# A window-attention and GELU block with its gradients on one core: gathers as plain loads, tokens in gather order, transposes moved between DMA and TensorE, and a new order

## The chip, the cores and the metric

One NeuronCore of a Trainium2 chip runs the whole program; the other cores are idle. The metric is the device time of one execution in microseconds (us), as the median of several runs. Beside it stands one execution that the hardware profiler recorded; every duration below comes from that one.

The engines are TensorE (PE, matrix products and transposes, results in PSUM), VectorE (DVE), ScalarE (ACT), GpSimd (POOL) and SyncE (SP, which here only issues DMA transfers). Each engine executes its own instructions strictly in order and waits on semaphores where it needs another's result.

## The reference

The reference computes a transformer block on 2048 tokens of width 512, and its vector-Jacobian product against a given `grad_out`. Everything is bfloat16.

```
ln1 = layernorm(x)                               # no scale, no shift
q, k, v = ln1 @ wqkv                             # 32 heads of 16
logits[s, w] = q[s] . k[s - 2 w] / 4             # w = 0..7: 8 keys, 2 apart, masked below 0
o[s] = sum_w softmax(logits[s])[w] * v[s - 2 w]
h  = x + o @ wo
h2 = h + gelu_tanh(layernorm(h) @ w1 + b1) @ w2 + b2     # F = 1792
return h2, and the gradients of x, wqkv, wo, w1, b1, w2, b2 against grad_out
```

So there is a forward pass (attention, then feed-forward), the backward pass through both, and the weight gradients, which are sums over all 2048 tokens.

## The kernel before, in words

The tokens are cut into four chunks of 512 (c = 0..3). The tensors of a chunk stand in SBUF either token-major (tokens on the 128 partitions) or feature-major (features on the partitions, 512 tokens along the free axis). The program is written as Python functions that record operations (`op`), each with an engine, a planned duration and what it reads and writes. `pl.emit(ORDER, HOMES)` then emits them in the order of a table of numbers, `ORDER`, made offline by a planner from the planned durations and from transfer rates (`DMA_RATE` and the like); `HOMES` is a table of memory addresses. Within an engine the order is therefore fixed, and it is not the order of the code.

- *Forward, attention.* `layernorm` (L315 to L335) normalises a chunk. `p1_proj` (L523) and `p1_v` (L540) project it to q, k and v. `dots` (L400) makes on DVE a product of 128x4096 elements, and TensorE sums it over each head with products of 32 columns (L408). After the softmax, `gather` (L389) fetches for each of 128 partitions 18 neighbouring rows of v, as an indirect DMA on POOL's queue with an index tile `rowi`; partition p then holds a run of tokens with its window. `band` multiplies (L427, DVE, 128x4096 again, `prbo`), sums on TensorE (L436) and writes with ACT (L441, `ost`). The outcome stands in *gather order*: partition p holds tokens 16 apart in groups of four. `unperm` (L451) transposes it on TensorE and puts the tokens back in order while ACT copies it out (L270). `p1_h` (L631, L638) applies `wo` and adds x.
- *Feed-forward.* `p2_h` (L660, L662), the derivative of GELU (`p2_dg`, L683 to L691, mostly DVE), `p2_out` (L706), and `p2_bwd` (L731, L733, L745 and `ln_bwd` L466 to L475). `goT`, the feature-major `grad_out`, and `w1T`, `w2T` come by transposing DMA from DRAM (`xload`, L264).
- *Backward, attention.* `p3_go` transposes the gradient of h on TensorE (L356, `ghT`, out by ACT), multiplies it by the transposed `wo` (L766, `got`) and turns the outcome back to token-major on TensorE (L378), from where it goes to DRAM (`go_d`). `p3_dots` is `dots` again (`prb`), and `p3_bands` runs `gather` and `band` three more times per chunk: `Rq` with `prbq`, `Rv` with `prbv` (which gathers `go_d`), `Rk` with `prbk`. `shift` (L799) copies coefficient rows with four small DMAs each. `p3_gl1` (L844) is the last product before the gradient of x.
- *Weight gradients* (`wg_ffn`, L872): 736 products that TensorE can run whenever their operands are there; the planner puts them between the other work.

Of the kernel before, what the change touches and what calls it, by code (L numbers as in the profile page):

```python
# [10 lines left out]
P = 128  # L11
BF16 = mybir.dt.bfloat16
# [15 lines left out]
DMA_RATE = 345.0  # L28
WIDE_RATE = 380.0
XPOSE_RATE = 215.0  # L30
XPOSE_SB = 170.0
# [27 lines left out]
class Op:  # L59
    __slots__ = ("i", "eng", "us", "lat", "fn", "bufs", "preds", "soft", "dma", "tag", "key", "piece", "stage", "mode", "cls")  # L60


class Plan:
# [21 lines left out]
    def op(self, eng, us, fn, r=(), w=(), dma=None, tag="", soft=(), piece=0.046, mode=0, cls=0, lat=None):  # L85
        o = Op()
        o.i, o.eng, o.us, o.fn, o.dma, o.tag = len(self.ops), eng, us, fn, dma, tag
        o.lat, o.piece, o.stage, o.mode, o.cls = lat, piece, self.stage, mode, cls
# [61 lines left out]
def kernel(  # L150
# [43 lines left out]
    def cst(name, shape, dt=BF16):  # L194
# [8 lines left out]
    mhalf = cst("mhalf", [P, TPC], F32)  # L203
    zrow = cst("zrow", [RPAD, D])
    rowi = cst("rowi", [P, 2], mybir.dt.uint32)
# [7 lines left out]
    ve1, ve2, nm1, nm2, rstd1, rstd2 = (cst(n, [P, NT], F32) for n in ("ve1", "ve2", "nm1", "nm2", "rstd1", "rstd2"))  # L213
    sg_, c0_, sx_ = (cst(n, [P, 2 * NT], F32) for n in ("sg", "c0", "sx"))

    v_t, k_t, q_t, go_t = ([dram.tile([RB, D], BF16, name=f"{n}_d{c}") for c in range(NC)] for n in ("v", "k", "q", "go"))
    ln1_t, o_t = ([dram.tile([CH, D], BF16, name=f"{n}_d{c}") for c in range(NC)] for n in ("ln1", "o"))
    ln2_t = [dram.tile([P, TPC, D], BF16, name=f"ln2_d{c}") for c in range(NC)]
    g_t, gh_t = ([dram.tile([F, CH], BF16, name=f"{n}_d{c}") for c in range(NC)] for n in ("g", "gh"))
    g3_t = [dram.tile([P, max(KEEP, 1), 4, D], BF16, name=f"g{n}_d") for n in "qkv"]  # L220

# [8 lines left out]
    IDENT, PMAT, SUM4, NSUM4, S32B, SMB, IND8, EMAT, MKB, MHALF, ZROW, ROWI = (fx(n, None) for n in (  # L230
        "ident", "pmat", "sum4", "nsum4", "s32", "sm", "ind8", "emat", "mk", "mhalf", "zrow", "rowi"))
    g3_d = [fx(f"g3{i}", t) for i, t in enumerate(g3_t)]
    v_d, k_d, q_d, go_d = ([fx(f"{n}{c}", t) for c, t in enumerate(ts)] for n, ts in (("v", v_t), ("k", k_t), ("q", q_t), ("go", go_t)))
    ln1_d, ln2_d, o_d = ([fx(n, t) for t in ts] for n, ts in (("ln1", ln1_t), ("ln2", ln2_t), ("o", o_t)))
    g_d, gh_d = ([fx(n, t) for t in ts] for n, ts in (("g", g_t), ("gh", gh_t)))
# [5 lines left out]
    GATHER = 7.0  # L241
# [12 lines left out]
    def load(dst, ap, src_ap, kb, r=(), key=None, tag="load", soft=(), row=1, q="SP"):  # L254
        return op(q, 0.5, lambda: (SY if q == "SP" else A).dma_start(out=ap(), in_=src_ap()), r=r, w=[(dst, key)],
                  dma=kb / (DMA_RATE if row == 1 else WIDE_RATE), tag=tag, soft=soft, piece=0.006 + 0.0385 * row, mode=4)

    def store(dst, ap, src, src_ap, kb, key=None, skey=None, q="SP", tag="store", row=1):
        e, us = (SY, 0.45) if q == "SP" else (G, 0.6)
        return op(q, us, lambda: e.dma_start(out=ap(), in_=src_ap()), r=[(src, skey)], w=[(dst, key)] if dst is not None else (),  # L260
                  dma=kb / (DMA_RATE if row == 1 else WIDE_RATE), tag=tag, piece=0.006 + 0.0385 * row, mode=5)

    def xload(dst, ap, src_ap, kb, r=(), key=None, tag="xload", soft=(), sb_src=False):
        return op("SP", 0.4, lambda: SY.dma_start_transpose(out=ap(), in_=src_ap()), r=r, w=[(dst, key)],  # L264
                  dma=kb / (XPOSE_SB if sb_src else XPOSE_RATE), tag=tag, soft=soft, piece=0.02, mode=3)

# [8 lines left out]

    def consts():
# [4 lines left out]
        op("DVE", 0.1, lambda: V.memset(mhalf[:], -0.5), w=[MHALF], tag="k")  # L281
        op("DVE", 0.27, lambda: V.memset(zrow[:], 0.0), w=[ZROW], tag="k")
        op("ACT", 0.25, lambda: A.copy(out=_sub(Pmat[:], [[1, 8], [8, DH]]), in_=_sub(ident[:], [[DH, 8], [1, DH]])), r=[IDENT], w=[PMAT], tag="k")
        for j in range(4):
            op("ACT", 0.2, lambda j=j: A.copy(out=S32[32 * j:32 * j + 32, :], in_=ident[32 * j:32 * j + 32, 32 * j:32 * j + 32]),
               r=[IDENT], w=[(S32B, j)], tag="k")
# [10 lines left out]
        for g in range(4):  # L297
            op("ACT", 0.2, lambda g=g: A.copy(out=Emat[:, g, 8 * g:8 * g + 8], in_=ind8[:]), r=[IND8], w=[EMAT], tag="k")
        op("POOL", 0.3, lambda: G.memset(mk[:], 0.0), w=[MKB], tag="k")
        for hf in range(2):  # L300
            op("POOL", 0.3, lambda hf=hf: G.affine_select(out=mk[:, hf], in_=mk[:, hf], compare_op=ALU.is_ge, fill=NEG, base=-2 * hf,
                                                          pattern=[[-4, 4], [0, 32]], channel_multiplier=1), w=[(MKB, hf)], tag="k")
        for w4 in range(4):
            for b_, o in ((0, 4 * w4), (1, 4 * (3 - w4))):
                op("POOL", 0.12, lambda w4=w4, b_=b_, o=o: G.iota(rowi[32 * w4:32 * w4 + 32, b_:b_ + 1], pattern=[[0, 1]], base=o * D,
                                                                 channel_multiplier=16 * D), w=[(ROWI, (w4, b_))], tag="k")

    def layernorm(c, src, MV, ST, VE, NM, R, mv, st, ve, nm, rs, dst, eng, tag, per=TPC):
        for g0 in range(0, TPC, per):
            js = range(g0, g0 + per)  # L310
            for j in js:
# [9 lines left out]
            op("DVE", 0.08, lambda s=s: V.tensor_scalar(out=ve[:, s], in0=mv[:, s, 1], scalar1=EPS, scalar2=None, op0=ALU.add),  # L321
               r=[(MV, t) for t in ts], w=[(VE, k)], tag="ve" + tag)
            op("POOL", 1.1, lambda s=s: G.tensor_tensor(out=rs[:, s], in0=ve[:, s], in1=mhalf[:, 0:per], op=ALU.pow), r=[(VE, k), MHALF],
               w=[(R, t) for t in ts], tag="pow" + tag)
# [3 lines left out]
            for j in js:  # L328
# [5 lines left out]
                else:  # L334
                    op("DVE", 0.31, lambda t=t, j=j: V.tensor_scalar(out=dst()[:, j, :], in0=src()[:, j, :], scalar1=mv[:, t, 0:1],  # L335
                                                                    scalar2=rs[:, t:t + 1], op0=ALU.subtract, op1=ALU.mult),
                       r=[(src, j), (R, t), (MV, t)], w=[(dst, j)], tag="norm" + tag)
# [5 lines left out]
    def to_fm_dma(src, dst, tag):  # L343
        xload(dst, lambda: _sub(dst()[:, 0, 0:1], [[P, 16], [1, P]]), lambda: src().rearrange("p j d -> p (j d)"), 512, r=[src], tag="fm" + tag,
              sb_src=True)
# [833 lines left out]
```

## Time and profile before

| what | number |
|---|---|
| median of three runs | 582.69 us (581.72 to 582.99) |
| the profiled execution, its own time | 582.41 us |
| its span, first to last instruction | 580.6 us |
| mean granted TensorE clock | 0.994 |
| TensorE busy | 554.3 us, 95% of the span |
| VectorE busy | 495.6 us, 85% |
| ScalarE busy | 340.9 us, 59% |
| GpSimd busy | 57.1 us, 10% |
| data moved by DMA | 133.31 MB |

The span leaves 1.8 us of the profiled execution's time outside it. "Busy" of TensorE contains modelled ends, so a busy TensorE may still have lost cycles; the distance from the start of one run of like instructions to the start of the next tells what one of them costs when nothing disturbs it. Rows of windows give for a stretch of time the busy time of each engine, the number of instructions in brackets, and the clock granted to TensorE (PEclk, 1.00 is full speed).

### The profile page before, as it was taken

To read this page: it belongs to the slowest core of one execution; us is meant where nothing else is said; L and a number is where in the kernel's file an instruction comes from. 1 tells how busy PE (TensorE), PEld (TensorE's weight loads), DVE (VectorE), ACT (ScalarE), POOL (GpSimd) and SP (SyncE) were. 2 spreads that over 40 slices of the span, in tenths; PEclk is the share of its full clock that TensorE was granted. 3 is DMA by queue.
4 is the path that set the end of the run, shared out by engine and by line. 5 is a ranking of instruction groups with operands and counts; after the bars stand their busy time and mean duration, and the time that the engine had idled before them with its cause. 6 is when DMAs were issued, how large, how long until landed. Compare 5 with 4: busy or idle time off the path is not lost.

```text
span 580.6 us, 9061 instructions
## 1 busy us (share of the span) xinstructions
PE 554.3 (95%) x3516; PEld 258.6 (45%) x3516; DVE 495.6 (85%) x649; ACT 340.9 (59%) x508; POOL 57.1 (10%) x67
## 2 busy tenths in 40 slices
PE   4989999799999998999999999999999999999997
PEld 1444444244444443444445445443444445544443
DVE  7789997889999999989997889899788996936824
ACT  5889699689975697669414455121552453542452
POOL 3010125030020113000001000010101001010000
PEclk9999999799999999999999999999999999999999
DMA  9787779688768936877977997869989896997653
GB/s 263 174 278 227 255 225 333 184 135 187 192 231 223 254 115 163 265 154 243 255 244 155 263 202 183 281 217 238 370 170 364 280 263 206 306 333 262 209 182 99
DMA packets 173467, 133.31 MB, mean 230 GB/s; under 512 B 116529, under 2 KB 167793, under 8 KB 171377
## 3 DMA queue, kind: packets, MB, share of 16 engines
q1 hardware_dynamic: 169488, 89.75, 60.0%
q0 software_dynamic: 3936, 42.99, 20.5%
q8 instruction: 27, 0.44, 0.3%
q14 instruction: 16, 0.12, 0.1%
HBM read 59.38 MB, written 42.93 MB: 176 GB/s over the span
## 4 chain that ended last, share of the span: by engine, by line
PE 50%; DVE 5%; DMA 3%; issue 1%; ACT 1%; SPq 1%; ACTq 0%; DVEq 0%
PE ps L872 22%; PE ps L844 7%; PE ps L745 4%; PE ps L731 3%; PE ps L436 3%; PE ps L766 2%; PE ps L706 2%; DMA Rk<-q_d,rowi 2%; DVE prbk L427 2%; PE ps L451 2%; PE ps L408 1%; PE ps L660 1%; DMA gw1in<-gh_d 1%; PE ps L378 1%; PE ps L356 1%
## 5 line engine op out<-in xcount | busy, mean ns | idle before, releaser
L660 PE MATMUL ps<-ln2T,w 128*128 128x512 bf16 x224 | 53.1, 379 | 0.5 <-DVE xb L733 0.2
L706 PE MATMUL ps<-w,gl 128*128 128x512 bf16 x224 | 52.5, 380 | 1.0 <-DVE h2s L708 0.7
L731 PE MATMUL ps<-goT,w2T 128*128 128x512 bf16 x224 | 52.8, 379 | 0.0
L872 PE MATMUL ps<-gw1in,ln2b 128*128 128x512 bf16 (+1 forms) x256 | 51.4, 353 | 0.9 <-DMA gw1in<-gh_d 0.9
L745 PE MATMUL ps<-w1T,xb 128*128 128x512 bf16 x224 | 50.6, 379 | 1.4 <-ACT gyr L466 1.4
L872 PE MATMUL ps<-gor,gw2in 128*128 128x512 bf16 x224 | 51.8, 379 | 0.0
L427 DVE TENSOR_TENSOR prbv<-Rv,cfv 128x4096 bf16<-128x4096 bf16 x16 | 35.9, 2284 | 17.6 <-DMA Rv<-go_d,rowi 13.9
L844 PE MATMUL ps<-wqkvT,gqkvT 128*128 128x512 bf16 x192 | 45.6, 379 | 0.3 <-ACT gqkvT L270 0.3
L662 ACT ACTIVATE xb<-ps,b1c 128x512 bf16<-128x512 f32 x56 | 35.6, 692 | 16.9 <-PE ps L660 15.2
L270 ACT CAST wgs<-ps 128x512 bf16<-128x512 f32 (+1 forms) x30 | 16.4, 566 | 49.5 <-PE ps L872 49.5
L427 DVE TENSOR_TENSOR prbq<-Rq,cfq 128x4096 bf16<-128x4096 bf16 x16 | 36.1, 2283 | 8.5 <-DMA Rq<-k_d,rowi 4.0
L427 DVE TENSOR_TENSOR prbk<-Rk,cfk 128x4096 bf16<-128x4096 bf16 x16 | 36.0, 2284 | 6.7 <-DMA Rk<-q_d,rowi 3.7
L427 DVE TENSOR_TENSOR prbo<-Ro,cfo 128x4096 bf16<-128x4096 bf16 x16 | 36.2, 2276 | 5.6 <-issue 4.9
L466 ACT ACTIVATE gyr<-ps,rstd 128x512 bf16<-128x512 f32 x32 | 21.8, 681 | 28.9 <-PE ps L844 15.7
L400 DVE TENSOR_TENSOR prf<-qt,kt 128x4096 bf16<-128x4096 bf16 x16 | 35.8, 2276 | 3.2 <-ACT qt L270 2.9
L733 DVE SCALAR_TENSOR_TENSOR xb<-xb,ps 128x512 bf16<-128x512 bf16 x56 | 36.8, 679 | 0.7 <-issue 0.2
L270 ACT COPY gqkvT<-ps 128x1024 bf16<-128x1024 bf16 x24 | 24.0, 1019 | 22.6 <-PE ps L451 9.2
L400 DVE TENSOR_TENSOR prb<-got,vw 128x4096 bf16<-128x4096 bf16 x16 | 36.0, 2284 | 0.7 <-PE ps L408 0.6
L872 PEld LDWEIGHTS <-ln2b 128*128 128x128 bf16 x256 | 24.2, 98 | 25.7 <-issue 3.0
L745 PEld LDWEIGHTS <-xb 128*128 128x128 bf16 x224 | 21.9, 98 | 27.7 <-issue 1.7
L706 PEld LDWEIGHTS <-gl 128*128 128x128 bf16 x224 | 21.5, 98 | 28.2 <-issue 3.0
L523 PE MATMUL ps<-ln1T,wqk 128*128 128x512 bf16 x128 | 32.8, 406 | 1.3 <-DMA wqk<-in_A_wqkv_dram 1.1
(170 smaller groups left out, 1009.1 us busy)
## 6 DMA issues: line engine op xcount, KB each, us to landing
g_d<-gl SPq DMA_DIRECT2D x12, 512.0 KB
gh_d<-xb SPq DMA_DIRECT2D x12, 512.0 KB
ln_d<-ln SPq DMA_DIRECT2D x8, 512.0 KB
w<-in_B_w_dram SPq DMA_DIRECT2D x2, 1792.0 KB
out_dram<-wgs SPq DMA_DIRECT2D x13, 256.0 KB
v_d<-tmv SPq DMA_DIRECT2D x8, 256.0 KB
k_d<-tmk SPq DMA_DIRECT2D x8, 256.0 KB
q_d<-tmq SPq DMA_DIRECT2D x8, 256.0 KB
```

The costliest lines, as they stand in the source:

```text
L270: fn = lambda: A.copy(out=ap(), in_=pap())
L400: op("DVE", tt_us(4096), lambda g=g, pr=pr: V.tensor_tensor(out=pr(), in0=ql()[:, g, :].unsqueeze(1).to_broadcast([P, W, 512]), in1=_sub(k ...
L427: V.tensor_tensor(out=pr().rearrange("p a j (d h) -> p a j d h", h=H), in0=_sub(R()[:, o0, 0:1], [[st, 2], [512, 4], [32, DH], [1, H]]), i ...
L523: T.matmul(ps()[:, gg * 512:(gg + 1) * 512], lhsT=wqk()[:, dc, sel * D + g * P:sel * D + (g + 1) * P], rhs=cols(st_[c]["ln1T"], dc, c in F ...
L660: T.matmul(ps(), lhsT=w1()[:, dc, f * P:(f + 1) * P], rhs=cols(ln2T[c], dc, c in FM2), start=(dc == 0), stop=(dc == DC - 1))
L662: op("ACT", act_us(512, 1), lambda f=f, ps=ps, xb=xb, f0=f0: A.activation(out=xb()[:, f - f0, :], in_=ps(), func=ACT.Identity, bias=b1c[:, ...
L706: T.matmul(ps(), lhsT=d["g"][f // 4]()[:, f % 4, j * P:(j + 1) * P], rhs=w2()[:, f, :], start=(f == 0), stop=(f == FT - 1))
L731: T.matmul(ps(), lhsT=w2T()[:, dc, f * P:(f + 1) * P], rhs=goT()[:, dc, :], start=(dc == 0), stop=(dc == DC - 1))
L733: op("DVE", 0.61, lambda f=f, ps=ps, z=z, f0=f0: V.scalar_tensor_tensor(out=z()[:, f - f0, :], in0=z()[:, f - f0, :], scalar=1.0, in1=ps() ...
L745: T.matmul(ps(), lhsT=d["d"][f // 4]()[:, f % 4, j * P:(j + 1) * P], rhs=w1T()[:, f, :], start=(f == 0), stop=(f == FT - 1))
L844: T.matmul(ps(), lhsT=d["gqkv"]()[:, b, j * P:(j + 1) * P], rhs=wqkvT()[:, b, :], start=(i == 0 and b == ks[0]), stop=(i == 2 and b == ks[ ...
L872: T.matmul(ps()[:, 0:N], lhsT=l, rhs=r, start=(n == 0), stop=(n == k - 1))
```

## The change

Line numbers in this section, where they differ, are those of the changed kernel.

- `gather` (L424) is a plain DMA on POOL's queue, whose source pattern names the 128 overlapping runs of 18 rows; the index tile and its eight `iota` are gone. The order of the partitions is mirrored in `dots` and `shift`.
- Tokens stay in gather order after the attention. `turn` (L484) does the same eight transposes as `unperm`, and ACT's copy behind them is contiguous. x is loaded a second time, in gather order (16 loads of 128 KB); `grad_out`, `ln1` and the stores of the outputs are cut in four pieces per chunk in that order; the reciprocal deviations of `ln1` are rearranged through DRAM (one store, four loads, four small DVE copies).
- `ghT`, the token-major gradient of the attention's output (`tmgod`) and `goT` are made by transposing DMA from SBUF to SBUF. 64 + 64 transposes on TensorE and 16 ACT copies of 1024 elements go.
- `w1T` and `w2T` are made by TensorE (`wturn`, L1057): 112 transposes and 14 ACT copies of 1024 elements; eight transposing loads go.
- `shift` is 32 ACT copies of 32 x 1024 elements in place of 32 DMAs.
- For the last chunk, g and the gradient of the hidden layer are transposed from SBUF to SBUF and do not pass through DRAM; the second copies of `ln1` and `ln2` are not stored and reloaded, and `KEEP` (chunks of attention gradients parked in DRAM) is 1 in place of 2.
- The first chunk's layernorm uses ACT's square root and a DVE reciprocal in place of POOL's power; half of its transposes are copied out by DVE.
- `warm` (L290) multiplies zeros 16 times, 128x512.
- The planner's rates are others, and `ORDER` and `HOMES` are new.

The first place is TensorE's queue near the start. Before: `wqk` and `wv` are the projections' weights, `Pmat` turns q to token-major.

```order
L523 LDWEIGHTS wqk_9_187
L523 MATMUL ps<-ln1T_69_10_196,wqk_9_187 128x512
...
L378 LDWEIGHTS qt_94_14_248
L378 MATMUL ps<-Pmat,qt_94_14_248 128x16x8
...
L540 LDWEIGHTS ln1T_69_10_196
L540 MATMUL ps<-wv_16_276,ln1T_69_10_196 128x512
```

After, the same place (`wz` is the tile of zeros; the last pair sums the first DVE product):

```order
L580 LDWEIGHTS ln1T_52_8_172
L580 MATMUL ps<-wv_9_179,ln1T_52_8_172 128x512
...
L397 LDWEIGHTS qt_88_14_234
L397 MATMUL ps<-Pmat,qt_88_14_234 128x16x8
L290 LDWEIGHTS wz_2_116
L290 MATMUL ps<-wz_2_116 128x512
...
L580 LDWEIGHTS ln1T_52_8_172
L580 MATMUL ps<-wv_9_179,ln1T_52_8_172 128x512
...
L440 LDWEIGHTS Emat
L440 MATMUL ps<-prf_16_318,Emat 32x512
```

The 16 products of zeros stand behind the 16 transposes of the first layernorm, 44 projection products and 8 transposes of q; four more products and the first sums follow.

The second place is POOL's queue in the forward attention. Before (`o_d` is the attention's output in DRAM):

```order
L389 DMA Ro_29_573<-v_d_57,rowi 128x9216
L260 DMA o_d_77<-ost_30_668 128x1x512
L389 DMA Ro_26_845<-v_d_58,rowi 128x9216
L323 TENSOR_TENSOR rstd<-ve,mhalf 128x4
L260 DMA o_d_77<-ost_30_668 128x1x512 x3
L389 DMA Ro_31_1108<-v_d_59,rowi 128x9216
L323 TENSOR_TENSOR rstd<-ve,mhalf 128x4
L260 DMA o_d_78<-ost_30_985 128x1x512 x2
```

After:

```order
L424 DMA Ro_14_368<-v_d_57 128x1x9216
L343 TENSOR_TENSOR rstd<-ve,mhalf 128x4
L266 DMA o_d_81<-ost_29_615 128x2048
L424 DMA Ro_27_859<-v_d_59 128x1x9216
L343 TENSOR_TENSOR rstd<-ve,mhalf 128x4
L424 DMA Ro_22_1060<-v_d_58 128x1x9216
L266 DMA o_d_83<-ost_25_1093 128x2048
```

The gathers stay on POOL's queue; chunk 2 is fetched ahead of chunk 1, and a chunk's output leaves in one store.

The third place is TensorE where the backward attention begins. Before (`prb` is the first backward product of DVE; `gw2in` feeds a weight gradient):

```order
L872 LDWEIGHTS gw2in_45_2668
L872 MATMUL ps<-gor_37_2874,gw2in_45_2668 128x512
L356 LDWEIGHTS ghr_1179_39_2944
L356 MATMUL ps<-ident,ghr_1179_39_2944 128x128
...
L872 LDWEIGHTS gw2in_45_2668
L872 MATMUL ps<-gor_44_2432,gw2in_45_2668 128x512
...
L408 LDWEIGHTS S
L408 MATMUL ps<-prb_36_3035,S 32x512
```

After:

```order
L957 LDWEIGHTS xw2in_41_2917
L957 MATMUL ps<-gor_42_2510,xw2in_41_2917 128x512
L841 LDWEIGHTS woT_46_2994
L841 MATMUL ps<-ghT_42_3278,woT_46_2994 128x512
...
L841 MATMUL ps<-ghT_45_3286,woT_46_2994 128x512
L440 LDWEIGHTS S
L440 MATMUL ps<-prb_45_3314,S 32x512
```

Ahead of the first sum of `prb` stood 28 products of weight gradients and 16 of `ghT` with `woT`; now 128 and 32 stand there. The number of TensorE products in the program is 3516 in both.

The core of the diff:

```diff
-DMA_RATE = 345.0
-WIDE_RATE = 380.0
-XPOSE_RATE = 215.0
-XPOSE_SB = 170.0
+DMA_RATE = 325.0
+WIDE_RATE = 337.0
+XPOSE_RATE = 180.0
...
+    def warm(n):
+
+        z = sb("wz", [P, 512])
+        pz = ps_("pwz")
+        op("DVE", 0.2, lambda: V.memset(z(), 0.0), w=[z], tag="wz")
+
+        def mm():
+            for _ in range(n):
+                T.matmul(pz(), lhsT=z()[:, 0:P], rhs=z(), start=True, stop=True)
+        op("PE", 0.2157 * n, mm, r=[z], w=[pz], tag="warm")
...
+            if per == 1:
+                op("ACT", 0.25, lambda s=s: A.activation(out=ve[:, s], in_=mv[:, s, 1], func=ACT.Sqrt, bias=epsc[:]), r=[(MV, t) for t in ts] + [EPSC],
+                   w=[(VE, k)], tag="sd" + tag, mode=7)
+                op("DVE", 0.08, lambda s=s: V.reciprocal(out=rs[:, s], in_=ve[:, s]), r=[(VE, k)], w=[(R, t) for t in ts], tag="rc" + tag)
...
+    def tm_dma(fm, off, dst, c, back, tag, pm):
+
+        st = sb("tm" + tag + "d", [P, 4, 512])
...
+            xload(st, lambda: _sub(st()[:, 0, 0:1], [[P, 16], [1, P]]), lambda: fm().rearrange("p g t -> p (g t)"), 512, r=[(fm, 0), (fm, 1)], tag="tmx" + tag)
+            store(dst[c], lambda: dst[c]()[r:r + CH, :].rearrange("(a p) (g d) -> p g a d", p=P, g=4), st,
+                  lambda: st().rearrange("p g (a d) -> p g a d", d=P), 720, key=0, tag="tmst" + tag, row=0.25)
...
-            G.indirect_dma_start(out=R().rearrange("p a d -> p (a d)"), out_offset=None,
-                                 in_=_ap(t[0:1, :], [[RW * D, RB // RW], [1, RW * D]]),
-                                 in_offset=bass.IndirectOffsetOnAxis(ap=rowi[:, int(back):int(back) + 1], axis=1),
-                                 element_offset=(RPAD - 14 if back else 0) * D)
...
+        op("POOL", 0.58, lambda: G.dma_start(out=R().rearrange("p a d -> p (a d)"), in_=_ap(d_b()[r0:r0 + 1, :], [[4 * D, 4], [16 * D, 32], [1, RW * D]])),
...
-        evict(dst, lambda: _sub(dst()[:, k0, 0:1], [[CH, 4], [16, 32], [1, 8]], 8 * mp), pt,
-              lambda: _sub(pt.bf(), [[256, 4], [1, 32], [32, 8]]), 1024, key=dkey, tag="un" + tag)
+        evict(dst, lambda: dst()[:, 2 * mp:2 * mp + 2, :], pt, lambda: pt.bf().rearrange("p (a n) -> p a n", a=2), 1024, key=mp, tag="un" + tag)
...
-        xload(goT, lambda: goT(), lambda: gof[c * CH:(c + 1) * CH, :], 512, tag="goT", soft=[(d["g"][1], None)])
...
+            load(gor, lambda j=j: gor()[32 * j:32 * j + 32], lambda ap=ap: ap, 128, key=j, tag="gor", soft=[(d["g"][1], None)])
+        to_fm_dma(gor, goT, "go")
...
+        if c in FMG:
+            to_fm_dma(gh_[c], ghT, "gh", soft=[(st_[NC - 1]["d"][2], None)])
...
+        if SHA:
+            for w4 in range(4):
+                op("ACT", act_us(1024), lambda w4=w4: A.copy(out=sh()[32 * w4:32 * w4 + 32],
...
+    def wturn(dst, dap, src, sap, kb, key, tag):
+
+        pt = ps_("ptw" + tag)
+
+        def tr():
+            for k in range(8):
+                T.transpose(pt.bf()[:, k * P:(k + 1) * P], sap(k), ident[:])
+        op("PE", 8 * XP, tr, r=[src, IDENT], w=[pt], tag="xp" + tag)
+        evict(dst, dap, pt, lambda: pt.bf().rearrange("p (a n) -> p a n", a=kb), 1024, key=key, tag="ev" + tag)
...
-KEEP = 2
+KEEP = 1
...
+WARM = 16
+FMG = (0, 1, 2, 3)
...
+SBX = ((0, 3), (1, 3))
+SHA = True
+W2PE = True
+W1PE = True
 ORDER = (
-    29, 25, 26, 4, 8, 11, 13, 12, 1, 9, 2, 6, 30, 32, 7, 79, 0, 20, 21, 22, 23, 5, 27, 56,
...
```

More of the change, by code (lines that the diff above doesn't have):

```diff
@@ L556, in p1_qkv @@
         p1_v(c)
-        to_tm_store(kt, PAD, k_d, c, True, "k", True)
-        to_tm_store(qt, 0, q_d, c, False, "q", True)
+        for fm, o, dd, back, n in ((kt, PAD, k_d, True, "k"), (qt, 0, q_d, False, "q")):
+            (tm_dma if (n, c) in TMD else to_tm_store)(fm, o, dd, c, back, n, c not in QKP)
     def p1_attn(c):
@@ L930 @@
     N2 = [["ACT"] * 4] * 4
+    warm(WARM)
     p1_load(0)
```

350 lines of the change are left out of this document (214 added, 136 removed), and 248 rows, old and new, of tables (HOMES, ORDER).

## The prediction, made before the changed kernel was run

> **What bounds the kernel now.** I read first the page's busy times, then the windows of a whole stage each, then the timeline of the one window that stood out, then the waits of the tiles that arrive by gather. The windows (start and end, length, then each engine's busy time; the last columns are the granted clock, the DMA share and GB/s):
>
> ```profile
> PE 554.3 (95%) x3516; PEld 258.6 (45%) x3516; DVE 495.6 (85%) x649; ACT 340.9 (59%) x508; POOL 57.1 (10%) x67
> ```
>
> ```profile
> 0.00:20.00 20.00, 11.31 (x45) 4.91 (x46) 13.77 (x45) 10.88 (x24) 6.78 (x22) 1.00 0.94 242
> 20.00:100.00 80.00, 75.84 (x598) 36.09 (x596) 76.45 (x72) 70.91 (x95) 15.54 (x10) 1.00 0.79 249
> 100.00:120.00 20.00, 16.04 (x109) 6.31 (x108) 15.76 (x18) 15.10 (x16) 1.74 (x1) 0.83 0.75 185
> 102.00:112.00 10.00, 6.04 (x53) 2.14 (x50) 8.06 (x6) 5.61 (x6) 0.00 (x0) 0.69 0.43 144
> 112.00:225.00 113.00, 112.76 (x595) 50.96 (x592) 108.99 (x186) 92.11 (x112) 16.97 (x17) 1.00 0.78 198
> 180.00:315.00 135.00, 132.43 (x658) 60.60 (x651) 125.12 (x239) 85.33 (x127) 9.74 (x10) 1.00 0.78 205
> 315.00:549.00 234.00, 231.35 (x1645) 110.79 (x1644) 194.01 (x149) 94.94 (x166) 17.45 (x18) 1.00 0.88 260
> 549.00:581.00 32.00, 27.58 (x163) 12.68 (x161) 12.75 (x30) 12.41 (x27) 0.00 (x0) 0.99 0.38 128
> ```
>
> TensorE is the bound over the whole (554.3 of 580.6 us), but not alone. From 20 to 315 us DVE is about as full (76.45 of 80, 108.99 of 113, 125.12 of 135), so there TensorE follows DVE and a delay of either moves the end. From 315 to 549 DVE has 40 us to spare (234 less 194.01), and only TensorE's work counts. The idle time of TensorE is 26.3 us: 8.69 at the start, 4.16 from 20 to 100, 3.96 from 100 to 120, some 5 in the middle, 4.42 at the end.
>
> One window is bad, 100 to 120. Its rows, POOL, DVE and TensorE (start, duration, line; in brackets the idle time before and what ended it):
>
> ```profile
> 60.18 1.14 POOL L389 DMA_INDIRECT Ro<-v_d,rowi  x1 [0.33 <-issue]
> 86.03 8.69 POOL L389 DMA_INDIRECT Ro<-v_d,rowi  x1 [8.64 <-PE ps L436]
> ```
>
> ```profile
> 96.73 2.28 DVE L400 TENSOR_TENSOR prf<-qt,kt 128x4096 bf16<-128x4096 bf16 x1
> 103.94 2.29 DVE L427 TENSOR_TENSOR prbo<-Ro,cfo 128x4096 bf16<-128x4096 bf16 x1 [4.93 <-issue]
> ```
>
> ```profile
> 106.88 1.21 PE L408 MATMUL ps<-prf,Emat 128*32 128x512 bf16 x8 [3.96 <-DVE h L638]
> ```
>
> The gather of chunk 2 takes 8.69 us on POOL where the one before took 1.14. So its rows land late, DVE stands 4.93 us, TensorE 3.96, and for ten microseconds its clock is granted at 0.69. DVE ran its 128x4096 products while POOL was held.
>
> What one instruction costs comes from starts in the tail, where TensorE runs undisturbed:
>
> ```profile
> 557.84 0.61 PE L451 MATMUL ps<-ident,gks 128*128 128x128 bf16 x8
> 558.28 1.03 PE L844 MATMUL ps<-wqkvT,gqkvT 128*128 128x512 bf16 x4
> ...
> 566.92 3.62 PE L872 MATMUL ps<-gq3in,rl 128*128 128x512 bf16 x16
> 570.37 1.89 PE L872 MATMUL ps<-gks,rl 128*128 128x512 bf16 x8
> ```
>
> Eight transposes take 0.44 us, 0.055 each; sixteen products of 128x512 take 3.45 us, 0.216 each.
>
> **The change part by part.** The sum is made against the profiled execution's 582.41 us; the median of the runs is 0.28 above it.
>
> *Gathers.* POOL's own rows:
>
> ```profile
> L389 POOL DMA_INDIRECT Ro<-v_d,rowi x4 | 12.0, 3006 | 46.6 <-PE ps L731 36.9 <-PE ps L436 8.6 <-POOL rowi L305 0.7
> L260 POOL DMA_DIRECT2D o_d<-ost x16 | 10.5, 669 | 49.2 <-ACT ost L441 49.2
> ```
>
> A plain DMA on POOL takes 0.67 us in the mean here, beside the same DVE products, and none of the sixteen is shown long. I take it that the plain gather does the same. Then chunk 2's rows are there in time, and the window from 100 to 120 loses what its neighbours lose. It loses 3.96 us idle and, at 0.69 clock over 6.04 us of work, about 1.9 more; the neighbour from 20 to 100 idles 4.16 in 80, so 1.05 in 20. Gain: 3.96 + 1.9 - 1.05 = 4.8. Bounds: 0, if the plain load is held likewise, and 5.9. The queue's order matters less: the twelve later gathers took about 1 us on POOL, off the path.
>
> [...]
>
> *Start.* Here is what the first projection waited for:
>
> ```profile
> 6.48 0.40 PE L356 MATMUL ps<-ident,ln 128*128 128x128 bf16 x2 [6.48 <-DVE ln L335]
> ...
> 11.17 9.93 PE L523 MATMUL ps<-ln1T,wqk 128*128 128x512 bf16 x32 [1.08 <-DMA wqk<-in_A_wqkv_dram]
> ```
>
> The layernorm loses four POOL powers and one of two ACT copies goes to DVE, but the last release was the weights' load, which the new order puts ahead of the later chunks' x. Gain 0.5, between -0.5 (the square root needs its table first) and 1.5.
>
> *Zeros.* The first 32 products took 9.93 us instead of 32 x 0.216 + 0.16 = 7.1: 2.9 are lost to a slow first stretch. The zeros stand behind these products, so they can't shorten it. They cost 16 x 0.216 = 3.45 us of TensorE. Cover would be DVE: it is nearly full from 20 us on, and TensorE idles 4.16 us up to 100. Loss: 1.0, bounds 0 and 3.45; if they delay the first sums and DVE's product buffers fill, it is the upper one. [...]
>
> *Transposes.* TensorE loses 128 and gains 112 of 0.055: 0.9 gained. ACT loses 16 copies of 1024 elements and gains 14, and 32 for `shift`:
>
> ```profile
> L270 ACT COPY gqkvT<-ps 128x1024 bf16<-128x1024 bf16 x24 | 24.0, 1019 | 22.6 <-PE ps L451 9.2
> ```
>
> 30 x 1.02 = 30.6 us; ACT goes from 340.9 to about 371 of 580, and most of it falls behind 315 us, where ACT works 94.94 of 234. Costed at 0. The eight DMA transposes for `ghT` and `tmgod` occupy SP for 1.9 us each:
>
> ```profile
> L264 SPq DMA_TRANSPOSE ln1T<-ln x3: 1938/1941/1957, 16.1 to 47.5; - x3
> ```
>
> Their cover is 100 products of weight gradients now placed ahead. The bytes fall: 7.3 MB for the last chunk's g and its gradient, 4 for `ln2`, 2 for `ln1`, 3 for one `KEEP`, less 2 for the second x, so some 14 of 133 MB. No term; it shortens landings if anything.
>
> *New order, first part (20 to 315 us).* Ahead of the first sum of `prb` stand 128 weight-gradient products and not 28, and 16 more products of `ghT`: 116 x 0.216 = 25 us of work that needs nothing of DVE, in the stretch where TensorE followed DVE. TensorE's idle time there, without the bad window, is about 4.16 + 0.24 + 2.57 = 7.0, and these fill it in part: I take 4.5. Bounds 0 and 7.0.
>
> *New order, second part (315 to 549).* The same 25 us, and the 72 transposes (4.0 us) that stood behind that point before, are missing there: the stretch shrinks from 234 to 205 us if TensorE sets it, beside DVE's 194. The slack of DVE falls from 40 to about 11 us. What it was spent on:
>
> ```profile
> L427 DVE TENSOR_TENSOR prbv<-Rv,cfv 128x4096 bf16<-128x4096 bf16 x16 | 35.9, 2284 | 17.6 <-DMA Rv<-go_d,rowi 13.9 <-ACT gyr L466 2.8 <-PE ps L436 0.9
> L427 DVE TENSOR_TENSOR prbq<-Rq,cfq 128x4096 bf16<-128x4096 bf16 x16 | 36.1, 2283 | 8.5 <-DMA Rq<-k_d,rowi 4.0 <-PE ps L436 3.8 <-PE ps L766 0.5
> L427 DVE TENSOR_TENSOR prbk<-Rk,cfk 128x4096 bf16<-128x4096 bf16 x16 | 36.0, 2284 | 6.7 <-DMA Rk<-q_d,rowi 3.7 <-issue 3.0
> ```
>
> DVE waited 21.6 us for gathers (13.9 + 4.0 + 3.7). Much of that was DVE running ahead, which it can't now. I take a loss of 2; bounds 0 and 15 (21.6 - 11, and some 4 for late transposes).
>
> Sum: 582.41 - 4.8 - 0.5 + 1.0 - 0.9 - 4.5 + 2.0 = 574.7, and 0.3 for the median: **575**.
>
> **The rivals.**
>
> *DVE binds the second part.* If all 21.6 us of waits stay and only 11 are free, 10.6 are lost in place of 2, and each late `ghT` or `go_d` adds: before, TensorE could turn these itself in 0.44 us per eight, now a transfer stands between two products, four times. With 15 lost: 588; with 20, 593. It turns the verdict from about 10 us of loss on, that is when DVE's waits behind 315 us pass some 20 us. For it speaks that waits of 21.6 were there with more slack; against it that fewer bytes move and that the last waits of TensorE in that stretch were only 2.65 us.
>
> *The plain load is held too.* The 4.8 fall away: 580, still faster. For it: the 8.69 us stood on POOL's queue, where the gathers remain. Against: the plain stores above.
>
> *All of it fits.* TensorE's idle time in the middle goes (7.0), the second part loses nothing, the zeros are covered: 582.7 - 5.9 - 1.0 - 0.9 - 7.0 = 568, or 564 with a better start and tail.
>
> *The change nets nothing.* Zeros fully paid (3.45), no gain from the order, 2 lost behind: 582.7 - 4.8 - 0.5 - 0.9 + 3.45 + 2 = 582, no change.
>
> **How the numbers follow.** Forecast (570 to 579) 0.46; the plain load held (579 to 581.5) 0.10; all fits (562 to 570) 0.07; nothing 0.05; DVE binds the second part (584 to 595) 0.32. 0.2%, 1.2 us, is about what a measurement of this kernel can tell from no change. Faster 0.46 + 0.10 + 0.07 = 0.63, same 0.05, slower 0.32. The range 563 to 592 leaves out a few per cent at the lower end and the worst third of the slower case; the forecast's own range is 570 to 579.
>
> **What would show it.** Right: no POOL row of a gather above 2 us; no window of 20 us with a clock under 0.95 between 20 and 560; TensorE's idle time from 20 to 315 under 4 us without the bad window; the zeros' 3.45 us with DVE not waiting behind them for `prf`; DVE's idle time behind 315 us near 11 and TensorE's there under 5. Wrong: TensorE waiting for `prb`, `prbq`, `prbv` or `prbk` by more than 5 us together, or for `ghT`; a gather of 8 us again; TensorE idle ahead of the zeros.

## The result, and the profile after

The changed kernel takes 977.03 us (974.38 to 984.64, four runs) where the kernel before took 582.21 us beside it: a ratio of 1.680, 95% interval 1.671 to 1.690. The prediction said 575, faster, with a range that ended at 592. It missed by 402 us, in sign and in size. In this section and the next, ratios and intervals leave out executions that ran at a lower clock than the others of the same kernel, while the times beside them are medians of all.

The page of the profiled execution (span 972.6 us) shows first that the engines' work hardly changed:

```profile
PE 585.1 (60%) x3516; PEld 264.4 (27%) x3516; DVE 498.7 (51%) x656; ACT 371.8 (38%) x541; POOL 29.8 (3%) x40
```

DVE is busy 498.7 us, as before (495.6); ACT 371.8, where 371 was forecast; TensorE 585.1 where it was 554.3, at a mean granted clock of 0.805 and not 0.994. So the 392 us by which the span grew are waiting. What DVE waited for (total, times, longest):

```profile
DVE prbv L459 <- DMA Rv<-go_d: 123.0, 4, 34.9
DVE prbq L459 <- DMA Rq<-k_d: 110.1, 4, 39.8
DVE prbo L459 <- DMA Ro<-v_d: 67.4, 2, 33.8
DVE prbk L459 <- issue: 40.9, 2, 36.0
```

It waited 300 us for three of the four kinds of gather alone, some 30 us at a time and up to 39.8. The page's list of DMA issues tells why (the last column is the median time from issue to landing):

```profile
Ro<-v_d POOLq DMA_DIRECT2D x4, 2304.0 KB, 43.5
Rq<-k_d POOLq DMA_DIRECT2D x4, 2304.0 KB, 47.9
Rv<-go_d POOLq DMA_DIRECT2D x4, 2304.0 KB, 42.9
Rk<-q_d POOLq DMA_DIRECT2D x4, 2304.0 KB, 45.1
```

A gather of 2304 KB lands in 43 to 48 us. In the kernel before it landed in about 10; here are the least, the median and the most of its `Ro` gathers:

```profile
DMA to landing us min/median/max: 10.2/10.3/17.8
```

The 17.8 is the gather that POOL held for 8.69 us. In the changed kernel the issue on POOL is as short as forecast (0.67 us each for the later ones); the transfer behind it is four times as long. While the first gather is in flight there is a stretch in which no compute engine of the core works at all. The windows of that stretch and of the two stages around it:

```profile
20.00:100.00 80.00, 45.94 (x370) 22.52 (x368) 40.24 (x40) 40.85 (x52) 3.22 (x4) 0.81 0.59 154
60.00:75.00 15.00, 0.00 (x0) 0.00 (x0) 0.00 (x0) 0.00 (x0) 0.00 (x0) 0.50 0.20 56
315.00:420.00 105.00, 104.80 (x486) 47.21 (x485) 94.19 (x177) 77.10 (x103) 2.36 (x1) 1.00 0.67 158
560.00:760.00 200.00, 73.24 (x427) 30.14 (x425) 57.28 (x37) 39.56 (x61) 3.85 (x6) 0.67 0.88 104
```

From 60 to 75 us every compute engine is at 0.00, and the 16 DMA engines are busy for a share of 0.20, moving 56 GB/s. A fifth of sixteen engines is the work of about three; the view is a mean and does not say which engines they are. Where no gather is needed, 315 to 420 us, TensorE is full (104.80 of 105). The backward attention, 560 to 760, has it busy 73 of 200 us.

The gather also holds transfers that have nothing to do with it. SP's queue and ACT at the first and the second gather:

```profile
35.27 40.22 SPq L261 DMA_DIRECT2D wo<-in_A_wo_dram  x1
```

```profile
138.25 1.01 ACT L276 CAST tmv<-ps 128x1024 bf16<-128x1024 f32 x1 [31.36 <-DMA q_d<-tmq]
```

SP stands 40.22 us on one issue, until the gather has landed, and with it everything behind it in SP's order. The length follows the gather: the same issue stands 28.03 us in k8, 10.85 in k128 and 9.54 in f_indirect, three of the kernels below. ACT waits 31.36 us until an unrelated store has left its tile. The rows show both delays; what makes these transfers wait for the gather they do not show.

One part did better than forecast. TensorE and DVE at the start:

```profile
9.28 5.81 PE L562 MATMUL ps<-ln1T,wqk 128*128 128x512 bf16 x16 [0.25 <-ACT ln1T L276]
```

```profile
16.88 2.26 DVE L432 TENSOR_TENSOR prf<-qt,kt 128x4096 bf16<-128x4096 bf16 x1
```

The first projection begins at 9.28 us (11.17 before) and DVE's first product at 16.88 (20.45 before).

### The profile page after: what moved, and what is told of

Same layout as the page of the kernel before. It is cut to its first block, busy times and chain, and to the rows that moved or that the text cites. A ratio compares the mean times of both kernels' runs of the same rounds, so it can differ in the third digit from the quotient of the medians.

```text
span 972.6 us, 9021 instructions
## 1 busy us (share of the span) xinstructions
PE 585.1 (60%) x3516; PEld 264.4 (27%) x3516; DVE 498.7 (51%) x656; ACT 371.8 (38%) x541; POOL 29.8 (3%) x40
## 4 chain that ended last, share of the span: by engine, by line
DMA 28%; PE 17%; SPq 7%; DVE 2%; issue 2%; ACT 0%; another core or an unknown queue 0%; DVEq 0%; POOLq 0%
DMA Rq<-k_d 10%; DMA Rv<-go_d 9%; PE ps L957 9%; SPq L270 6%; DMA ro<-o_d 5%; DMA Rk<-q_d 4%; PE ps L931 2%; DVE prbq L459 2%; PE ps L841 1%; PE ps L817 1%; PE ps L468 1%; PE ps L803 1%; PE ps L484 1%; SPq L266 1%; PE ps L440 0%
## 5 line engine op out<-in xcount | busy, mean ns | idle before, releaser
L957 PE MATMUL ps<-gw1in,ln 128*128 128x512 bf16 (+1 forms) x192 | 44.9, 383 | 63.7 <-DMA gw1in<-gh_d 63.7
L468 PEld LDWEIGHTS <-S 128*32 128x32 bf16 x512 | 12.0, 104 | 250.0 <-DVE prbo L459 66.9
L721 PE MATMUL ps<-ln2T,w 128*128 128x512 bf16 x224 | 56.8, 399 | 29.1 <-DMA ln2T<-ln 28.9
L468 PE MATMUL ps<-prbv,S 128*32 128x512 bf16 x128 | 12.2, 506 | 82.2 <-DVE prbv L459 82.2
L473 ACT ACTIVATE gvs<-ps 128x512 bf16<-128x512 f32 x16 | 9.4, 605 | 128.3 <-PE ps L468 128.3
L957 PEld LDWEIGHTS <-ln 128*128 128x128 bf16 x256 | 26.1, 105 | 92.4 <-issue 71.5
L468 PE MATMUL ps<-prbo,S 128*32 128x512 bf16 x128 | 11.1, 459 | 65.9 <-DVE prbo L459 65.9
L931 PE MATMUL ps<-wqkvT,gqkvT 128*128 128x512 bf16 x192 | 49.4, 399 | 0.0
L957 PE MATMUL ps<-gor,gw2in 128*128 128x512 bf16 x168 | 39.9, 379 | 1.9 <-DVE xb L805 1.9
L721 PEld LDWEIGHTS <-w 128*128 128x128 bf16 x224 | 21.9, 102 | 58.8 <-issue 37.4
## 6 DMA issues: line engine op xcount, KB each, us to landing
Ro<-v_d POOLq DMA_DIRECT2D x4, 2304.0 KB, 43.5
```

Of the source, the lines that this page charges most:

```text
L468: T.matmul(ps()[32 * j:32 * j + 32, :], lhsT=S32[:], rhs=pr()[:, hf, j, :], start=(hf == 0), stop=(hf == 1), skip_group_check=True)
L721: T.matmul(ps(), lhsT=w1()[:, dc, f * P:(f + 1) * P], rhs=cols(ln2T[c], dc, c in FM2), start=(dc == 0), stop=(dc == DC - 1))
L931: T.matmul(ps(), lhsT=gT()[:, j, b * P:(b + 1) * P], rhs=wqkvT()[:, k0 + b, :], start=(i == 0 and b == 0), stop=(i == 2 and b == 3))
L957: T.matmul(ps()[:, 0:N], lhsT=l, rhs=r, start=(n == 0), stop=(n == k - 1))
```

## The experiments

The question splits in two: what makes a gather four times slower, and what the rest of the change is worth without that. The edits below are to the changed kernel, to *f_indirect* (the changed kernel with the old gather) or to the kernel before, as each says. Ratios are to the kernel before, run on the same chip.

### What slows the gather

The suspect was the shape of the source pattern, `[[4*D, 4], [16*D, 32], [1, RW*D]]`: its outermost dimension counts 4. The rivals were the overlap of the runs in a plain load, and the new transposing DMAs.

*f_four*: the same load in four pieces, each with 32 outermost.

```diff
-G.dma_start(out=R(), in_=_ap(d_b()[r0:...], [[4*D, 4], [16*D, 32], [1, RW*D]]))
+for a in range(4):
+    G.dma_start(out=R()[32*a:32*a+32], in_=_ap(d_b()[r0+4*a:...], [[16*D, 32], [1, RW*D]]))
```

> The changed kernel with each gather cut into four plain loads of 32 partitions, whose outermost source dimension is 32 and not 4; everything else stays. Theory A (a load is spread over no more DMA engines than its outermost dimension counts, so 4 of 16 here): the last of the four lands within 10 to 13 us, DVE's waits for gathers fall from 303 us to under 30, and the time is 565 to 585 us. Theory B (plain loads whose runs overlap are slow however they are written): landing stays above 35 us, time above 900. Theory C (the new transposing DMAs starve the gathers): landing above 30 us, time above 850.

*f_indirect*: the old way of fetching, in the new order of partitions.

```diff
-G.dma_start(out=R(), in_=_ap(d_b()[r0:...], [[4*D, 4], [16*D, 32], [1, RW*D]]))
+G.indirect_dma_start(out=R(), in_=_ap(d_b(), [[RW*D, RB//RW], [1, RW*D]]),
+                     in_offset=IndirectOffsetOnAxis(ap=rowi[:, 0:1], axis=1), element_offset=r0*D)
```

> The changed kernel with the indirect gather put back in the new partition order; everything else stays. A and B: landing near 10 us, time 565 to 585 us, and POOL may again be held for 8 us once or twice. C: landing stays above 30 us, time above 850.

*k8* and *k128*: the changed kernel, where only the counts of the pattern differ.

```diff
-[[4 * D, 4], [16 * D, 32], [1, RW * D]]
+[[4 * D, 8], [32 * D, 16], [1, RW * D]]     # k8
+[[4 * D, 128], [1, RW * D]]                 # k128
```

> The plain load of the changed kernel with 8 as its outermost source dimension and 16 behind it: the same bytes from the same 540 rows, but the tokens reach other partitions, so the attention's outputs are others. A: landing near 21.5 us, half of 43, and a time of 640 to 760 us. B and C: landing stays at 40 to 48 us, time 950 to 1000.

> The plain load of the changed kernel with 128 as its outermost source dimension, neighbouring partitions 4 rows apart: the same bytes from the same rows, other tokens on the partitions, so the attention's outputs are others. Theory A (as many engines as the outermost dimension allows, 16 at most): landing 10 to 13 us and a time of 585 to 597 us, like the indirect gather. Theory B (plain loads of overlapping runs are slow): landing above 20 us, time above 650.

*b_plain4*: the kernel before, with nothing of the change but this load.

```diff
-G.indirect_dma_start(out=R(), ..., in_offset=IndirectOffsetOnAxis(ap=rowi[:, int(back):int(back)+1], axis=1), ...)
+G.dma_start(out=R(), in_=_ap(t[r0:r0+1, :], [[4*D, 4], [16*D, 32], [1, RW*D]]))
```

> The kernel before with the changed kernel's plain load and nothing else of the change; the partitions of the gathers of v and k come in mirrored order, so the outputs are others. A and B: landing near 43 us and a time of 850 to 1050 us. C: landing near 10 us, time 575 to 590.

What was measured. The landing of the `Ro` gathers (least, median, most), in order for the changed kernel, b_plain4, k8, k128 and f_indirect:

```profile
DMA to landing us min/median/max: 42.8/43.5/46.5
```

```profile
DMA to landing us min/median/max: 42.1/44.7/47.2
```

```profile
DMA to landing us min/median/max: 24.4/27.3/30.2
```

```profile
DMA to landing us min/median/max: 8.9/9.7/11.6
```

```profile
DMA to landing us min/median/max: 9.7/10.0/16.9
```

| kernel | outermost count | landing of `Ro`, median us | time, us |
|---|---|---|---|
| changed | 4 | 43.5 | 977.03 |
| b_plain4 | 4 | 44.7 | 940.36 (one run) |
| k8 | 8 | 27.3 | 765.36 (one run) |
| k128 | 128 | 9.7 | 589.19 (one run) |
| f_indirect | indirect | 10.0 | 591.24, ratio 1.0136 (1.0085 to 1.0187) |
| f_four | 32, four pieces | 10.2 each piece | 639.71, ratio 1.101 (1.0936 to 1.1084) |

The same bytes from the same rows land in 43.5, 27.3 and 9.7 us as the outermost count goes from 4 to 8 to 128. Overlapping runs are no hindrance (k128 has them, and lands in 9.7 us where the indirect gather takes 10.0), and the new transposes are not the cause (f_indirect has them all, b_plain4 none). The order of the rows is no cause either: the indirect gather fetches them in the changed kernel's order. Put into the kernel before, this load alone costs 357 us (one run).

How many engines carry the gather can be read where its queue has little beside it. In the changed kernel, from 60 to 75 us, POOL's queue takes 17.9% of the time of the 16 engines and moves 0.83 MB; in k8, from 45 to 60 us, it takes 44.6% and moves 1.38 MB. That is the work of 2.9 engines at count 4 and of 7.1 at count 8: both stay under the count. In the same 15 us count 8 moves only 1.7 times the bytes, as a busy engine moves less there (some 13 GB/s where it was 19). So at 8 the landing is above the 21.5 us that the theory gave, and the count of engines is not all of it.

Theory A goes with the traces as far as they reach: 2.9 engines' work at count 4, 7.1 at count 8, and landings in that order (43.5 to 9.7 is a factor of 4.5, 43.5 to 27.3 one of 1.6). By what rule a transfer gets its engines, and how many carry the gather of k128, is not shown.

f_four missed its forecast: its pieces land in 10.2 us in the median, but up to 16.5, and the kernel takes 640 us. The queue that carries the gathers (packets, MB, share of 16 engines' span), for f_four, f_indirect and k128:

```profile
q0 software_dynamic: 4080, 41.42, 28.9%
```

```profile
q0 software_dynamic: 3312, 41.42, 19.3%
```

```profile
q0 software_dynamic: 3312, 41.42, 19.0%
```

The same 41.42 MB cost 28.9% of 637.2 us, 184 us of all engines, in pieces of 32 partitions, and 113 and 112 us in whole tiles of 128. So a piece of 32 partitions is a slow shape too; why was not tried.

### What the rest of the change is worth

f_indirect is the rest of the change. Its forecast was 565 to 585 us, and the prediction's sum had a gain of 8 us for the whole change; it loses 8 (1.36%). Its windows:

```profile
0.00:20.00 20.00, 12.78 (x54) 5.61 (x56) 17.07 (x49) 12.13 (x27) 4.02 (x15) 1.00 0.79 239
20.00:100.00 80.00, 69.75 (x585) 34.29 (x589) 63.79 (x64) 64.87 (x82) 5.91 (x6) 0.96 0.75 220
100.00:120.00 20.00, 19.62 (x147) 8.44 (x147) 19.96 (x16) 19.61 (x29) 0.58 (x1) 1.00 0.91 309
180.00:315.00 135.00, 132.30 (x610) 60.16 (x619) 120.03 (x229) 95.31 (x124) 6.24 (x2) 1.00 0.68 163
400.00:450.00 50.00, 46.81 (x348) 21.20 (x353) 44.18 (x29) 28.40 (x40) 4.14 (x5) 1.00 0.99 284
450.00:500.00 50.00, 46.91 (x331) 21.64 (x335) 41.80 (x38) 24.38 (x44) 4.58 (x5) 1.00 0.92 306
```

The bad stretch from 100 to 120 us is cured: TensorE 19.62 of 20 at a granted clock of 1.00. The start gains 1.5 us. But from 20 to 100 TensorE idles 10.2 us and not 4.2, and from 400 to 500 6.3 and not 1.8 (by the windows of before, 98.23 of 100 busy). These figures of f_indirect are upper ones, as its trace has 3463 of the 3516 products. Six suspects were tried.

*The zeros.* Edits of f_indirect: `WARM = 16` to 1 (i_one_zero), and the op moved to the head of TensorE's queue (i_zeros_first).

```diff
-WARM = 16
+WARM = 1                  # i_one_zero
 ORDER = (
-    10, 6, 12, 17, ...    # op 1, the zeros, is the 126th
+    10, 6, 12, 17, ...    # i_zeros_first: op 1 stands right behind op 0, the tile's memset
```

> The changed kernel with the indirect gather, and one product of zeros in place of 16. If the zeros are paid for where they stand, 15 x 0.216 = 3.2 us go and the time is 587 to 589 us; if DVE covers them, as the prediction took for the larger part, 590 to 592.

> The changed kernel with the indirect gather, and the 16 products of zeros at the head of TensorE's queue, ahead of the first transposes. If they warm the clock there, the first 16 projection products take near 3.6 us and not 5.8, and with the 3.45 us gone from their old place the time is 585 to 588; if they only delay the transposes, the first projection starts 1 to 2 us later than 9.3 us and the time stays at 590 to 592.

i_one_zero: 589.86 us, ratio 1.0108 (1.0047 to 1.0170). That is 1.6 us less than f_indirect by the ratios, far inside their intervals, so what the zeros cost where they stood, from nothing to their full 3.45 us, stays open. i_zeros_first: 586.71 us, 1.0063 (1.0032 to 1.0093), some 4 us better than f_indirect (1 to 8 by the intervals). TensorE's first rows in f_indirect, then in i_zeros_first:

```profile
9.40 5.86 PE L570 MATMUL ps<-ln1T,wqk 128*128 128x512 bf16 x16 [0.25 <-ACT ln1T L277]
```

```profile
2.23 6.28 PE L291 MATMUL ps<-wz 128*128 128x512 bf16 x16 [2.23 <-DVE wz L287]
...
10.05 3.61 PE L570 MATMUL ps<-ln1T,wqk 128*128 128x512 bf16 x16 [0.65 <-ACT ln1T L277]
```

At the head, the zeros take the slow first stretch on themselves (6.28 us for sixteen), and the first sixteen projections take 3.61 us and not 5.86. They start 0.65 us later. That it is the clock which makes the first stretch slow is not shown: from 0 to 20 us the granted clock stands at 1.00 in both runs.

*b_zeros*: the same for the kernel before; no other edit. The zeroed memory of `Sm` serves as operand.

```diff
+def zeros():
     V.memset(Sm[:], 0.0)
+    for _ in range(16):
+        T.matmul(raw[:, 7*BANK:8*BANK], lhsT=Sm[:, 0, :], rhs=Sm[:].rearrange("p a b -> p (a b)"), start=True, stop=True)
```

> The kernel before with 16 products of a zero tile (the memory of Sm) at the head of TensorE's queue and nothing else. The first 32 projection products should take 7.1 us and not 9.9, as the zeros at the head did in the changed kernel for its first 16 (3.61 us for 5.86). If the start is on the path, the time falls by 2 to 3 us, to 580 to 581; if DVE and ACT set the start, it stays within 1 us of 583.

581.13 us, ratio 0.9969 (0.9943 to 0.9995). It is the only kernel of these with the reference's work that beats both, by 0.3%, just outside the interval. Its first 32 projections take 7.2 us and not 9.9 (two, a short pause, then thirty in 6.64), and DVE's first product starts at 18.51 us and not at 20.45.

*The first gather.* In f_indirect it lands in 16.9 us and TensorE waits for its product:

```profile
57.83 2.75 PE L476 MATMUL ps<-prbo,S 128*32 128x512 bf16 x24 [6.76 <-DVE prbo L467]
```

Two of the transfers beside it were suspected. Each was moved away alone, by its place in `ORDER`:

```diff
-... 532 (load of w1) ahead of the first prbo ...
+... 532 behind the first prbo ...              # i_w1_late
-... 562 (store of rstd1, 4-byte pieces) ...
+... 562 behind the fourth product of h ...     # i_r_late
```

> The changed kernel with the indirect gather, and the load of w1 (1792 KB) moved behind the first product of the first gathered rows in SP's order. Theory F (the first gather lands in 16.9 us and not 10 because w1 shares the DMA engines with it): landing falls to 10 to 12 us, TensorE's wait of 6.8 us near 51 us falls under 2, and the time falls by 4 to 7 us, to 584 to 587. Theory G (the store of the deviations in pieces of 4 bytes, issued 2 us behind the gather, is what holds it): landing stays at 15 us or more and the time within 2 us of 591.

> The changed kernel with the indirect gather, and the store of the reciprocal deviations (2048 pieces of 4 bytes) moved some 60 us later in SP's order; w1 stays. G: landing of the first gather falls to 10 to 12 us and the time to 584 to 587 us. F: landing stays at 15 us or more, time within 2 us of 591.

Either cures the landing (10.1 and 10.9 us at most), so neither F nor G alone was right: it takes both transfers to hold the indirect gather. In k128 both stand beside the plain load with 128 outermost, and it lands in 11.6 us at most. None of the three brings time: ratios of 1.0149 (1.0121 to 1.0177) in i_w1_late, 1.0151 (1.0093 to 1.0210) in i_r_late, and one run of 589.19 us in k128. In i_w1_late the wait only changes its place, and the edit itself does that, as `w1` now comes later:

```profile
59.65 1.04 PE L1065 MATMUL ps<-ident,w 128*128 128x128 bf16 x8 [5.80 <-DMA w<-in_B_w_dram]
```

*The shifts*, back on SP in f_indirect.

```diff
-SHA = True
+SHA = False
```

> The changed kernel with the indirect gather, and the 32 shifts as small DMAs on SP again and not as ACT copies. If ACT had room, as the prediction took it, the time stays within 2 us of 591, or rises where SP is late; if the 32 us of ACT are paid for in part, it falls by 3 us or more.

602.53 us, ratio 1.0325 (1.0286 to 1.0364): 11 us worse. In this order ACT is the better place, and by far. On SP, DVE waits 14.30 us in one place for a 64-KB transfer. SP's last issue of one before the wait ends stands at 409.59 us, right behind the issue of a transposing load (`gw1in`) that took 7.47 us:

```profile
412.10 1.23 DVE L877 TENSOR_TENSOR glf<-ps,attn 128x1024 bf16<-128x1024 f32 x1 [14.30 <-DMA shk<-glf]
```

*DVE in the second part.* This was the prediction's main rival: DVE binds it. Half of each backward product was left out, in f_indirect and in the kernel before.

```diff
-V.tensor_tensor(out=pr(), in0=R rows [[st, 2], [512, 4], ...], in1=cf [[128, 2], [32, 4], ...])
+V.tensor_tensor(out=pr()[:, 0], in0=R rows [[512, 4], ...], in1=cf [[32, 4], ...])     # tags q, v, k
```

> The changed kernel with the indirect gather, where DVE makes only half of each product in the three backward gathers (128x2048 and not 128x4096; the sums read that half twice, so the gradients of wqkv and x are others). 48 x 1.14 = 55 us of DVE go from the second part, TensorE's work stays. Theory D (DVE binds the second part of the new order): the time falls by 8 us or more, to 575 to 583. Theory E (the loss lies in the first 100 us and in landings): it falls by under 3 us.

> The same halving in the kernel before. With 40 us of slack in DVE both theories expect a fall of 0 to 4 us; D expects it to be smaller than in the run beside it by 5 us or more, E expects the two falls to be alike.

i_half: 590.51 us, 1.0121 (1.0059 to 1.0182), two runs; b_half: ratio 1.0034 (0.9982 to 1.0085). Taking 55 us of work from DVE brings nothing that the intervals can tell from zero, in either kernel. Theory D asked for 8 us or more and falls. What DVE waited for the gathers behind 315 us in f_indirect (total, times, longest) is 11.2 us, not the 20 of that rival:

```profile
DVE prbq L467 <- DMA Rq<-k_d,rowi: 8.7, 3, 3.8
DVE prbv L467 <- DMA Rv<-go_d,rowi: 2.5, 2, 1.3
```

*The DMA engines in the second part*, 0.99 busy from 315 to 450 us in f_indirect. The transposing loads for the weight gradients of the feed-forward became plain loads of the same bytes.

```diff
-xload(Gs[c], lambda: G_(), lambda: dts[c][f0*P:f1*P, :], ...)
+load(Gs[c], lambda: G_().rearrange("p a b -> p (a b)"), lambda: dts[c][f0*P:f1*P, :].rearrange("(p r) t -> p (r t)", p=P), ...)
```

> The changed kernel with the indirect gather, where the loads of g and of its gradient for the weight gradients (gw2in, gw1in) are plain loads of the same bytes and not transposing ones, so that out_4 and out_6 are others; TensorE, DVE and ACT do the same work. Theory H (the rest of the loss is the DMA engines, full of transposes from 315 to 500 us): their share falls from 1.0 to under 0.7 there and the time falls by 5 us or more, to 578 to 586. Theory I (the engines' order itself loses the time): it stays at 588 to 592.

> The same in the kernel before. H: it has more work of TensorE behind the gathers to cover a late transfer, so the fall is 0 to 3 us and smaller than in the run beside it by 3 us or more. I: both stay within 2 us.

1.0095 (1.0064 to 1.0127) and 0.9941 (0.9919 to 0.9963): a fall of 2.4 us against f_indirect, inside the intervals, and of 3.4 us in the kernel before, clear of them. But the share of the DMA engines fell only to 0.86 from 315 to 450 us and 0.93 from 450 to 500, not under 0.7 as the forecast had it, so theory H was not put to its full test. What was tested speaks against it: the same relief gave the kernel before no less, so these transposes do not explain the difference.

*The length of the backward gathers.* They fetch 9 of their 18 rows, and DVE reads those twice.

```diff
-G.indirect_dma_start(out=R(), in_=_ap(d_b(), [[RW*D, RB//RW], [1, RW*D]]), ...)
+n = RW if tag == "o" else RW // 2
+G.indirect_dma_start(out=R()[:, 0:n], in_=_ap(d_b(), [[n*D, RB//n], [1, n*D]]), ...)
-o0 = (2 if sgn < 0 else 0) + 4 * m
+o0 = (2 if sgn < 0 else 0) + (4 * m if tag == "o" else 0)
```

> The changed kernel with the indirect gather, where the twelve backward gathers fetch 9 of their 18 rows and DVE's products read those rows over again (the gradients of wqkv and x are others); every product, sum and copy keeps its size. A gather should land in some 6 us and not 10. Theory J (the second part is a chain of buffer free, gather, product, sum, and 10 us of landing are on it): the time falls by 5 us or more, to 586 or less. Theory K (the loss is in the order of TensorE, DVE and ACT among themselves): it stays within 2 us of 591.

> The same in the kernel before. J: its gathers have more of TensorE's work beside them, so the time falls by 0 to 3 us, less than in the run beside it by 3 us or more. K: both stay within 2 us.

i_short: 581.47 us, 0.9968 (0.9945 to 0.9991). b_short: 578.04 us, 0.9910 (0.9876 to 0.9944). The landing of `Rq` in i_short, and TensorE's window from 450 to 500:

```profile
DMA to landing us min/median/max: 6.0/7.8/10.9
```

```profile
450.00:500.00 50.00, 49.52 (x353) 23.96 (x359) 43.36 (x38) 27.12 (x47) 6.97 (x5) 1.00 0.84 254
```

Against f_indirect the time falls by 1.7%, 9.8 us (6 to 13 by the intervals), for 2 to 3 us less of landing in each of twelve gathers (medians of 7.8 to 8.5 us, where 6 was forecast); TensorE is busy 49.52 of 50 where it was 46.91. The kernel before gains 0.9%, 5.3 us, more than either theory gave it, though its landings fell no less. So the gathers are on the path in both, and cost about 4.5 us more in the new order (1 to 8 by the intervals): theory J, for a good half of the 8 us if that figure is right.

What stays open: the remaining 3 us or so, for which the zeros (3.45 us at most) are the only candidate that was tried, and why the time that the first gather gave back in i_w1_late and i_r_late was gone at the end. The gathers at half length also took bytes from the DMA engines (106.61 MB against 120.76). That the latency and not the load of the engines did it is argued, not shown: by the shares of the queues i_gw_plain took some 27 us of all engines' time away and gained 2.4 us, i_short some 35 us and gained 9.8.

## Why the prediction was wrong, point by point

- *Gathers, the step that failed.* "I take it that the plain gather does the same" was said of the issue on POOL (0.67 us), and the issue did behave so. That the transfer behind it keeps its 10 us was not even a term of the sum: the landing was taken over from the indirect gather, its change put at nothing, without a bound from any row. It became 43 to 48 us, sixteen times, because the source pattern had 4 as its outermost count, and that is nearly all of the loss: 977 against 591 with the indirect gather.
- *The gain of 4.8 there.* The bad window from 100 to 120 us went, but with the indirect gather still in place (f_indirect, 19.62 of 20 busy; its longest POOL row of a gather 2.74 us). The rest of the change did it, not the plain load. Every trace of the order before that fetches indirectly has the long issue (8.68 to 8.70 us in five kernels), and no trace of the new order has an issue of a gather above 2.82; which part of the order decides it is not shown. The rival "the plain load is held too" asked about the right step and the wrong part of it: no issue of a plain gather on POOL took over 1.05 us.
- *Start, 0.5.* Too small: 1.9 us at the first projection, 3.6 us at DVE's first product. How much of it reached the end was not measured.
- *Zeros, 1.0 lost where they stand.* Not settled by i_one_zero (1.6 us, inside the noise). That they can't shorten the slow first stretch from there was right: the first sixteen products took 5.86 us in f_indirect. With the zeros at the head they took 2.25 us fewer, and the kernel before gained 0.3%.
- *Transposes, 0.9.* Not tried alone. That ACT has room for `shift` was right, and its opposite costs 11 us.
- *Order, first part, a gain of 4.5.* Wrong in sign: TensorE's idle time from 20 to 315 us, without the bad window, was to fall from 7.0 to 2.5 and is 13.8 in f_indirect. The rise lies from 20 to 100 us, from 4.2 to 10.2, 6.8 of it behind the first gather. The new order puts two more transfers beside that gather; with `w1` moved away TensorE waits for `w1` instead.
- *Order, second part, a loss of 2; and the rival at 588.* f_indirect at 591 lies near the rival's number, but not by its mechanism: halving DVE's products there changed nothing. From the first sum of `prb` to the end f_indirect takes 233.4 us and the kernel before 256.8: 23.4 less. The forecast had 29 us of work gone from there and a loss of 2, so that term was too small: the loss is nearer 6. What grew is the price of the gathers, 9.8 us by i_short beside 5.3 before.
- *The range.* It held no case in which a transfer itself is slower. A change of how a 2304-KB transfer is described had to have such a case, with the landing's share of the path as its price: each of the sixteen gathers landed some 34 us later than in f_indirect, and 24 us of that reached the end (386 us over sixteen).

## What to carry to other kernels

When a DMA is rewritten, price its landing and not only its issue, and look first at the outermost count of its access patterns: 4 in the source here made a 2304-KB load land in 43.5 us where 128 made it 9.7, and beside it one issue on SP's queue stood 40.22 us. A plan made from planned durations is worth no more than they are; the table here was laid out for a gather that took 6.4 us and got one of 43. To learn what binds a stage, take away one thing at a time in both kernels: here half of DVE's backward products brought nothing, and gathers of half the length brought 10 us.

## What the runs showed of the hardware that was not expected

- A plain load of 2304 KB in one DMA landed in 43.5, 27.3 and 9.7 us with an outermost source count of 4, 8 and 128. In 15 us with little else on the DMA engines, the first kept 2.9 of 16 busy and the second 7.1; with every compute engine idle all DMA of the core moved 56 GB/s beside the first.
- While the first ran, one issue on SP's queue stood for 40.22 us (10.85 with a count of 128), and beside the second gather a store issued from SP kept ACT waiting 31 us for its tile.
- The same bytes in four loads of 32 partitions cost the DMA engines 184 us in place of 112.
- An indirect gather that lands in 10 us beside one extra transfer, be it a load of 1792 KB or a store of 2048 pieces of 4 bytes, took 16.9 us beside both; a plain load with 128 outermost took 11.6 beside both.
